# Attention and two dense layers on one core: two shared buffers for the raw rows of q, k and v, and phi written in place

## The chip, the core and the metric

The kernel runs on one core of a Trainium2 chip. The core has TensorE (PE in the profile; PEld are its weight loads), VectorE (DVE), ScalarE (ACT), GpSimd (POOL) and SyncE (SP), which here issues nearly all transfers, one after the other in a fixed order. Each engine works through its own list of instructions in order; an instruction that waits holds up all that stand behind it on that engine. The metric is the device time of one execution in microseconds (us).

## The reference

```python
B, H, S, D = 4, 8, 576, 64            # q, k, v: float32
scores = softmax(causal(q @ k.T / sqrt(D)))          # per batch and head
local  = scores @ v
q_p    = phi(q)                        # phi(x) = x + 1 for x > 0, exp(x) otherwise
mem    = (q_p @ M_prev) / (q_p . z_prev + 1e-6)
x      = g * mem + (1 - g) * local     # g = sigmoid(beta), per head
x      = x.transpose(0, 2, 1, 3).reshape(2304, 512)
h      = softplus(x @ w_in)  @ w_out   # 512 -> 2048 -> 512, weights float64
out    = relu(h @ w2_in) ** 2 @ w2_out # 512 -> 2048 -> 512, weights float64
```

All inputs but the float64 weights are float32. The kernel keeps every operand of a product as two 16-bit halves, a high one and a low one (the rest), and makes each product of three partial ones.

## The kernel before

The 2304 tokens are cut into 18 chunks of 128 (`NC`, `CH`): two batches run in turn, 4 chunks of each, and the two last half chunks of the pair form one mixed chunk; so chunks 0 to 8 are the first pair, 9 to 17 the second. Within a chunk the heads are taken in groups (`steps`), fewer groups where the row of scores is short.

For each chunk raw rows of k, q and v are loaded from HBM by SyncE (`load`, 256 KB each) and prepared. `prep_k`: ScalarE copies to 16 bits (L226), VectorE makes the low half (L227), a transposing transfer issued by SyncE writes `KT` (L193). `prep_q` does the same for `qT` (L217, L218), `prep_v` makes `V` without a transpose (L234, L235), and `prep_phi` makes `phi(q)` (L251, L252, L254) and its halves (L256, L257) and has them transposed into `phiT`. There are nine buffers each for `KT` and `V` (`KVB`), two each for `qT` and `phiT`. Raw rows of q, of k and of v have one buffer each; a second one, in another pool, holds the raw k of chunk 1. A raw row can be loaded once the row before it in its buffer has been used.

The attention of a group: scores on TensorE (L309), a VectorE reduction with the mask (L314), Exp on ScalarE (L318), the probabilities split into halves (L330 on ScalarE, L331 on VectorE) in one of two tiles `p16`, and transposed by a transfer into `PT` (L193; in chunks 0 and 1 TensorE transposes). Then TensorE multiplies with `M` (L346) and `V` (L354) into the one tile `pvt`, which VectorE scales (`xt`, L374; the tile has the tag `prod`, one buffer, which the first half of `prep_phi` uses too, as `phie`), adds (L381) and splits (L386, `xn`) into x, again transposed.

The first dense layer needs x of two chunks (a block of 256 tokens). Its weights come in 32 pieces of 512 KB (`wst`, three buffers), which VectorE turns from float64 to float32 and splits with four instructions each (L417, L418, L419, L422) and ScalarE with one (L421). `unit_h` makes 24 products (L434 to L436) and softplus (ScalarE L438 to L440, L444; VectorE L441, L445); `unit_xq` and `unit_x` the second product (L451 to L453, L496 to L498). These units are interleaved with the attention steps, by the costs in `unit_time` and `step_cost`. The second layer follows when attention is done; its weights are loaded and split in the same way from then on (`w34_to`).

The order of the instructions on every engine is fixed when the kernel is built: a scheduler takes ready work by priority (`tc.high_priority` raises attention and weights; the preparation of chunks has none) along a modelled timeline, in which a tile's buffers and their users count. So a change of buffers moves instructions on all engines.

Of the kernel before, what the change touches and what calls it, by code (L numbers as in the profile page):

```python
# [8 lines left out]
F32 = mybir.dt.float32  # L9
# [8 lines left out]
P = 128  # L18
# [20 lines left out]
NST = 3  # L39
PTB = 4  # L40
PB = 2
P16 = 2
ST2 = 4

# [2 lines left out]
def kernel(  # L47
# [16 lines left out]
    B, H, S, D = q.shape  # L64
# [46 lines left out]
    att = att_cm.__enter__()  # L111
# [4 lines left out]
    stage = stage_cm.__enter__()  # L116
# [18 lines left out]

    p16 = [att.tile([P, 2 * EMAX], F16, name=f"p16_{i}") for i in range(P16)]
    zero = stage.tile([P, P], F16, name="zero", bufs=1)
# [22 lines left out]
    raw, qT, phiT, KT, V, Mt, Pt, PT, pvt, cs_t = ({} for _ in range(10))  # L160

    def segs(g):
        x = CH[g]
        if len(x) == 2:
            return [(x[0], P * x[1], 0, P)]
        return [(2 * x[0] + i, 4 * P, i * R, R) for i in range(2)]

    def lo_eng(g):
        return dve if g < LOE else pool

    def load(nm, g, pool_=None):
        if g >= NC or (nm, g) in raw:
            return
        src = {"q": q, "k": k, "v": v}[nm]
        t = (pool_ or att).tile([P, H, D], F32, name="raw" + nm, bufs=1)
        for b, s0, r0, n in segs(g):
            sp.dma_start(out=t[r0:r0 + n], in_=src[b, :, s0:s0 + n, :].rearrange("h p d -> p h d"))
        raw[nm, g] = t
    def load_m(g):
        for b, s0, r0, n in (segs(g) if g < NC else []):  # L180
            if s0 == 0:
                t = att.tile([P, EMAX], F32, tag="Pt", name="mraw", bufs=PB)[:, :HD].rearrange("p (h d) -> p h d", h=H)
                for i in range(2):
# [3 lines left out]
    def transp(g, out, in_, lim):  # L187
        nblk = in_.shape[1] // P
        if g >= lim:
            step = nblk if nblk <= 12 else nblk // 2  # L190
            for a in range(0, nblk, step):
                e = a + step
                sp.dma_start_transpose(out=out[:, a:e], in_=in_[:, a * P:e * P])  # L193
            return
        for a in range(0, nblk, 8):
            e = min(nblk, a + 8)
            ps = mm.tile([P, 8, P], F16, tag="mm", name="tps")
            for i in range(a, e):
                pe.transpose(ps[:, i - a], in_[:, i * P:(i + 1) * P], ident)
            act.activation(out[:, a:e], ps[:, :e - a], AF.Copy)  # L200
# [47 lines left out]
    def prep_phi(g):  # L248
        r = raw.pop(("q", g))
        e = att.tile([P, H, D], F32, tag="prod", name="phie")  # L250
        act.activation(e, r, AF.Relu, scale=-1.0)  # L251
        act.activation(e, e, AF.Exp, scale=-1.0)  # L252
        f = att.tile([P, H, D], F32, name="phi")
        dve.scalar_tensor_tensor(f, r, 0.0, e, ALU.max, ALU.add)  # L254
        fn = att.tile([P, H, 2, D], F16, name="phin")
        act.activation(fn[:, :, 0, :], f, AF.Copy)  # L256
        lo_eng(g).tensor_tensor(fn[:, :, 1, :], f, fn[:, :, 0, :], ALU.subtract)  # L257
        phiT[g] = att.tile([P, H, P], F16, name="phiT", bufs=2)
        transp(g, phiT[g], fn.rearrange("p h t d -> p (h t d)"), TP)
# [24 lines left out]
    def emit_s(g, h0):  # L284
        G, ext = GRP[g], EXT[g]
        p = att.tile([P, EMAX], F32, name="Pt", bufs=PB)
        if h0 == 0:
# [219 lines left out]


    load("k", 0)
    load("q", 0)  # L510
    load("k", 1, stage)
    load("v", 0)
    gates()
    z_setup()
# [5 lines left out]
    def prep_part(g, part):  # L520
        if g >= NC:
            return
        if part == 0:
            prep_k(g)
            load("k", g + 1)
        elif part == 1:
            prep_q(g)
        elif part == 2:
            prep_phi(g)
            load("q", g + 1)  # L530
        elif part == 3:
            prep_v(g)
            load("v", g + 1)
            prep_m(g)
            load_m(g + 1)

    prep_k(0)
    prep_q(0)
    prep_phi(0)
    load("q", 1)  # L540
    prep_v(0)
# [344 lines left out]
```

## Time and profile before

| | us |
|---|---|
| median of 3 runs (976.44 to 980.92) | 976.58 |
| profiled execution, whole | 977.68 |
| its span, first to last instruction | 975.9 |
| PE busy | 884.2 (91%) |
| DVE busy | 668.0 (68%) |
| ACT busy | 587.2 (60%) |

The span is what the trace covers; the rest of the profiled execution, 1.8 us, lies around it. Busy shares are averages over stages: in the first tenth of the span PE is less than half busy, after it over nine tenths. A wait is idle time of an engine in front of an instruction, put down to what ended last of all that this instruction waited for; with engines that work in order, the work named can itself have been late for another reason, which its own wait shows. A DMA share of 1 means that on average all 16 DMA engines had packets under way; as packets overlap, it can pass 1.

### The profile page before, as it was taken

The page shows a single profiled execution, that of the slowest core. Times are in us where ns is not written, and L with a number is a line of the kernel's source. Part 1 is how long each engine was busy: PE and PEld are TensorE (multiplying, and loading weights), DVE is VectorE, ACT ScalarE, POOL GpSimd, SP SyncE. Part 2 cuts the span into 40 slices and gives each one's busy share as a digit, 9 for nine tenths or more (in the row PEclk, how much of TensorE's full clock was granted, in tenths as well). Part 3 has the DMA queues.
Part 4 walks back from the last instruction along what each step waited for, and adds up shares of the span by engine and source line. Part 5 has one row for each costly group of instructions (what it writes and reads, how often), then busy time and mean ns, then how long its engine had stood idle before and what let it go on. Part 6 is the DMA issues. An engine that isn't in the chain of part 4 may idle for free.

```text
span 975.9 us, 21791 instructions
## 1 busy us (share of the span) xinstructions
PE 884.2 (91%) x8994; PEld 680.1 (70%) x9012; DVE 668.0 (68%) x1437; ACT 587.2 (60%) x1094; POOL 2.2 (0%) x10
## 2 busy tenths in 40 slices
PE   4345898889998899999999999999999999999998
PEld 3234787778877788888888888544684585486483
DVE  7998998877748677675846499998894075066050
ACT  7765878768649687775937556562274065056051
POOL 0000000000000000000000000000000000000000
PEclk8555999999999999999999999999999999999999
DMA  9999989755699976646554375620000000000000
GB/s 232 224 241 215 214 162 195 118 95 112 99 159 176 160 125 104 104 83 108 94 88 80 64 234 172 211 65 22 22 2 11 33 1 4 30 12 1 33 12 22
DMA packets 283219, 101.05 MB, mean 104 GB/s; under 512 B 248048, under 2 KB 280816, under 8 KB 283120
## 3 DMA queue, kind: packets, MB, share of 16 engines
q1 hardware_dynamic: 282880, 99.65, 51.3%
q8 instruction: 70, 1.15, 0.5%
q14 instruction: 29, 0.24, 0.1%
q10 hardware_dynamic: 240, 0.02, 0.0%
HBM read 48.78 MB, written 4.72 MB: 55 GB/s over the span
## 4 chain that ended last, share of the span: by engine, by line
PE 60%; DMA 16%; DVE 13%; ACT 6%; issue 3%; SPq 1%; ACTq 0%; DVEq 0%
DMA PT<-p 8%; PE ops L829 7%; PE ops L827 6%; PE ops L828 6%; PE h2ps L801 4%; PE h2ps L799 4%; PE h2ps L800 4%; DMA rawq<-in_q_dram 3%; PE xps L452 3%; PE xps L451 3%; PE xps L453 3%; PE s_ps L309 3%; PE pvt L354 2%; PE hps L436 2%; PE hps L435 2%
## 5 line engine op out<-in xcount | busy, mean ns | idle before, releaser
L434 PE MATMUL hps<-x,W 128*128 128x256 f16 x576 | 157.8, 276 | 3.2 <-DVE cc L273 3.0
L435 PE MATMUL hps<-x,W 128*128 128x256 f16 x576 | 158.4, 276 | 1.7 <-ACT x L477 1.7
L436 PE MATMUL hps<-x,W 128*128 128x256 f16 x576 | 158.2, 275 | 0.0
L452 PE MATMUL xps<-g,W 128*128 128x256 f16 x512 | 138.5, 273 | 1.7 <-DVE g L445 1.7
L453 PE MATMUL xps<-g,W 128*128 128x256 f16 x512 | 138.7, 273 | 0.0
L451 PE MATMUL xps<-g,W 128*128 128x256 f16 x512 | 137.5, 273 | 1.1 <-DVE spa L441 0.7
L318 ACT ACTIVATE Pt<-Pt,cs 128x128 f32<-128x128 f32 (+4 forms) x144 | 84.2, 585 | 67.4 <-DVE cs L314 67.4
L309 PE MATMUL s_ps<-KT,qT 128*128 128x128 f16 (+2 forms) x992 | 83.9, 225 | 36.6 <-DVE cs L314 35.9
L829 PE MATMUL ops<-W,gg 128*128 128x512 f16 x288 | 108.5, 379 | 0.9
L827 PE MATMUL ops<-W,gg 128*128 128x512 f16 x288 | 109.2, 379 | 0.1
L828 PE MATMUL ops<-W,gg 128*128 128x512 bf16 x270 | 102.3, 379 | 0.0
L309 PEld LDWEIGHTS <-qT 128*128 128x128 f16 (+1 forms) x992 | 59.8, 105 | 48.5 <-issue 43.7
L331 DVE TENSOR_TENSOR p<-Pt,p 128x512 f16<-128x512 f32 (+2 forms) x104 | 69.3, 667 | 29.6 <-ACT p L330 28.8
L831 ACT ACTIVATE osb<-ops 128x512 f32<-128x512 f32 x18 | 10.8, 597 | 123.4 <-PE ops L829 123.4
L808 DVE TENSOR_TENSOR r<-h2ps,r 128x512 f32<-128x512 f32 (+1 forms) x16 | 10.0, 623 | 108.0 <-PE h2ps L801 107.2
L354 PE MATMUL pvt<-V,PT 128*128 128x64 f16 (+1 forms) x1392 | 60.7, 197 | 19.5 <-DMA PT<-p 18.3
L314 DVE CUSTOM_DVE_ANT_0 Pt<-s_ps,mask 128x128 f32<-128x128 f32 (+3 forms) x128 | 62.0, 485 | 18.6 <-PE s_ps L309 17.9
L354 PEld LDWEIGHTS <-PT 128*128 128x128 f16 (+1 forms) x1392 | 50.3, 104 | 28.7 <-DMA PT<-p 25.1
L330 ACT ACTIVATE p<-Pt 128x512 f16<-128x512 f32 (+2 forms) x104 | 63.1, 606 | 11.2 <-DMA PT<-p 10.2
L435 PEld LDWEIGHTS <-W 128*128 128x128 f16 x576 | 56.9, 99 | 10.2 <-issue 3.6
L799 PE MATMUL h2ps<-XT,WS 128*128 128x256 f16 (+1 forms) x256 | 63.7, 259 | 0.0
L800 PE MATMUL h2ps<-XT,WS 128*128 128x256 f16 (+1 forms) x256 | 63.7, 259 | 0.0
(160 smaller groups left out, 2076.5 us busy)
## 6 DMA issues: line engine op xcount, KB each, us to landing
wst<-in_moe_w_in_dram SPq DMA_DIRECT2D x32, 512.0 KB, 5.0
wst<-in_moe_w_out_dram SPq DMA_DIRECT2D x32, 512.0 KB, 4.7
rawk<-in_k_dram SPq DMA_DIRECT2D x16, 256.0 KB, 4.3
rawq<-in_q_dram SPq DMA_DIRECT2D x16, 256.0 KB, 3.9
rawv<-in_v_dram SPq DMA_DIRECT2D x16, 256.0 KB, 4.7
out_dram<-osb SPq DMA_DIRECT2D x16, 256.0 KB, 2.0
PT<-p SPq DMA_TRANSPOSE x100, 3.4
mraw<-in_M_prev_dram SPq DMA_DIRECT2D x8, 128.0 KB, 3.7
```

The source lines that it names most:

```text
L309: pe.matmul(o[x * n:(x + 1) * n], qT[g][:, t * H + h, x * n:(x + 1) * n], KT[kb][:, h, a - j * P:e - j * P], start=(t == 0), stop=(t == 1),)
L354: pe.matmul(o[r], t[:, o0 + i + y, r], V[kb][:, z, h, :], start=(i == 0 and y + z == 0), stop=(i == nb - 1 and y > 0),)
L434: pe.matmul(o, wh, x[:, c], start=(c == 0), stop=False)
L435: pe.matmul(o, wh, x[:, NCC + c], start=False, stop=False)
L436: pe.matmul(o, wl, x[:, c], start=False, stop=(c == NCC - 1))
L451: pe.matmul(ps, wh, gh, start=(f == f0), stop=False)
L452: pe.matmul(ps, wh, gl, start=False, stop=False)
L453: pe.matmul(ps, wl, gh, start=False, stop=(f == f1 - 1))
L799: pe.matmul(o, wh, xh, start=(k == 0), stop=False)
L827: pe.matmul(ps, gh, W4[0][:, f, :], start=(a == 0), stop=False)
L828: pe.matmul(ps, gh, W4[1][:, f, :], start=False, stop=False)
L829: pe.matmul(ps, gl, W4[0][:, f, :], start=False, stop=(a == NFC - 1))
```

## The change

Raw rows of q, k and v are allocated from one tag with two buffers (`RAWB`), in the order in which the program asks for them: k0, q0, k1, v0, q1, v1, and then k, q, v of each chunk. Each load takes the buffer of the raw row two places earlier and waits until that one has been used. The extra buffer for the raw k of chunk 1 is gone. `phi` is written over its input `phie`, so the buffer of the tag `prod` stays taken until both halves of phi are made, and not only until phi is. All else is as it was.

```diff
--- before.py
+++ after.py
@@ -39,6 +39,7 @@
 NST = 3
 PTB = 4
 PB = 2
+RAWB = 2
 P16 = 2
 ST2 = 4
 
@@ -168,11 +169,11 @@
     def lo_eng(g):
         return dve if g < LOE else pool
 
-    def load(nm, g, pool_=None):
+    def load(nm, g):
         if g >= NC or (nm, g) in raw:
             return
         src = {"q": q, "k": k, "v": v}[nm]
-        t = (pool_ or att).tile([P, H, D], F32, name="raw" + nm, bufs=1)
+        t = att.tile([P, H, D], F32, tag="raw", name="raw" + nm, bufs=RAWB)
         for b, s0, r0, n in segs(g):
             sp.dma_start(out=t[r0:r0 + n], in_=src[b, :, s0:s0 + n, :].rearrange("h p d -> p h d"))
         raw[nm, g] = t
@@ -250,7 +251,7 @@
         e = att.tile([P, H, D], F32, tag="prod", name="phie")
         act.activation(e, r, AF.Relu, scale=-1.0)
         act.activation(e, e, AF.Exp, scale=-1.0)
-        f = att.tile([P, H, D], F32, name="phi")
+        f = e
         dve.scalar_tensor_tensor(f, r, 0.0, e, ALU.max, ALU.add)
         fn = att.tile([P, H, 2, D], F16, name="phin")
         act.activation(fn[:, :, 0, :], f, AF.Copy)
@@ -508,7 +509,7 @@
 
     load("k", 0)
     load("q", 0)
-    load("k", 1, stage)
+    load("k", 1)
     load("v", 0)
     gates()
     z_setup()
```

What the change does to the lists of instructions (line numbers of the changed kernel are one higher from `RAWB` on).

SyncE, around the transposes of the first probabilities (`PT`) of chunk 2; `wst` are weight pieces. Before:

```order
36 L193 DMA_TRANSPOSE KT<-kn 128x8x128
37 L193 DMA_TRANSPOSE PT<-p_1_102 128x8x128
38 L177 DMA rawv<-in_v_dram 128x8x64
39 L177 DMA rawk<-in_k_dram 128x8x64
40 L401 DMA wst<-in_moe_w_out_dram 128x4x128
41 L193 DMA_TRANSPOSE PT<-p_0_101 128x8x128
42 L401 DMA wst<-in_moe_w_out_dram 128x4x128
43 L177 DMA rawq<-in_q_dram 128x8x64
44 L177 DMA rawv<-in_v_dram 128x8x64
45 L193 DMA_TRANSPOSE KT<-kn 128x8x128
46 L177 DMA rawk<-in_k_dram 64x8x64 x2
47 L398 DMA wst<-in_moe_w_in_dram 128x4x128
```

Now:

```order
36 L194 DMA_TRANSPOSE KT<-kn 128x8x128
37 L194 DMA_TRANSPOSE PT<-p_1_102 128x8x128
38 L402 DMA wst<-in_moe_w_out_dram 128x4x128
39 L194 DMA_TRANSPOSE qT<-qn 128x8x128 x2
40 L194 DMA_TRANSPOSE PT<-p_0_101 128x8x128
41 L178 DMA rawv<-in_v_dram 128x8x64
42 L399 DMA wst<-in_moe_w_in_dram 128x4x128 x2
43 L194 DMA_TRANSPOSE phiT<-phin 128x8x128
44 L194 DMA_TRANSPOSE PT<-p_1_102 128x8x128
45 L178 DMA rawk<-in_k_dram 128x8x64
46 L399 DMA wst<-in_moe_w_in_dram 128x4x128
47 L194 DMA_TRANSPOSE PT<-p_0_101 128x8x128
```

Before, raw v of chunks 6 and 7 and raw k of chunks 7 and 8 (two halves) stood here among the transposes; now it is raw v of chunk 4 and raw k of chunk 5, and one weight piece more. Over the whole list up to the transposed x of chunk 2, SyncE issues raw k for 11 chunks before and 7 now, raw v for 10 and 6, raw q for 6 and 6, `KT` transposes 7 and 4, weight pieces 22 and 25.

VectorE, at the first evaluation of softplus (`spa`, L441 before, L442 now) and behind it; `xt` is scaled attention output, `phin` the low half of phi. Before:

```order
236 L418 SCALAR_TENSOR_TENSOR wcv<-wst,wcv 128x512
237 L254 SCALAR_TENSOR_TENSOR phi<-rawq,phie 128x512
238 L372 TENSOR_TENSOR cc<-cc,gP 128x4
239 L418 SCALAR_TENSOR_TENSOR wcv<-wst,wcv 128x512
240 L273 TENSOR_SCALAR cc<-nps 128x2x4
241 L419 SCALAR_TENSOR_TENSOR wcv<-wst,wcv 128x512
242 L441 SCALAR_TENSOR_TENSOR spa<-hps,spa 128x512
243 L314 ISA Pt,cs<-s_ps,mask 128x384
244 L314 ISA cs 128x1
245 L374 TENSOR_TENSOR xt<-pvt,cc 128x512
246 L419 SCALAR_TENSOR_TENSOR wcv<-wst,wcv 128x512
247 L257 TENSOR_TENSOR phin<-phi,phin 128x8x64
```

Now (the row of phi itself, L255, stands four rows ahead of the first one shown):

```order
245 L423 TENSOR_TENSOR W_69<-wcv,W_68 128x4x128
246 L371 TENSOR_SCALAR cc<-cs 128x4
247 L276 TENSOR_TENSOR cc<-cc,gM 128x2x4
248 L332 TENSOR_TENSOR p_1_102<-Pt,p_1_102 128x2x256
249 L258 TENSOR_TENSOR phin<-phie,phin 128x8x64
250 L420 SCALAR_TENSOR_TENSOR wcv<-wst,wcv 128x512
251 L418 TENSOR_SCALAR wcv<-wst 128x512
252 L315 ISA Pt,cs<-s_ps,mask 128x384
253 L315 ISA cs 128x1
254 L372 RECIPROCAL cc<-cc 128x4
255 L446 TENSOR_TENSOR g_0_888<-spa,g_0_887 128x512
256 L375 TENSOR_TENSOR xt<-pvt,cc 128x512
```

Before, `xt` stood between phi and `phin`; now it follows `phin`. The first L441 has 243 instructions ahead of it in both lists; among them are 8 fewer of L227 and L235 now (halves of k and v), 7 more on weights, 1 fewer of L331, 3 more for q (L218 to L220), and small ones. The low half of x of chunk 1 (L386), on which the first dense unit waits, is instruction 209 before and 211 now: 6 fewer halves of k and v and 7 more on weights stand ahead of it, and one small one of 4 columns.

SyncE once more, where the second pair of batches begins, at the transposed x of chunk 10. Before:

```order
166 L193 DMA_TRANSPOSE x_2699<-xn 128x8x128
167 L193 DMA_TRANSPOSE KT<-kn 128x8x128
168 L177 DMA rawq<-in_q_dram 128x8x64
169 L177 DMA rawv<-in_v_dram 128x8x64
170 L177 DMA rawk<-in_k_dram 128x8x64
171 L193 DMA_TRANSPOSE qT<-qn 128x8x128 x2
172 L177 DMA rawv<-in_v_dram 128x8x64
173 L193 DMA_TRANSPOSE PT<-p_1_102 128x8x128
174 L193 DMA_TRANSPOSE KT<-kn 128x8x128
175 L177 DMA rawk<-in_k_dram 64x8x64 x2
176 L177 DMA rawv<-in_v_dram 64x8x64 x2
177 L193 DMA_TRANSPOSE phiT<-phin 128x8x128
```

Now:

```order
168 L194 DMA_TRANSPOSE x_2692<-xn 128x8x128
169 L178 DMA rawv<-in_v_dram 128x8x64
170 L194 DMA_TRANSPOSE qT<-qn 128x8x128 x2
171 L178 DMA rawk<-in_k_dram 128x8x64
172 L194 DMA_TRANSPOSE PT<-p_1_102 128x8x128
173 L178 DMA rawq<-in_q_dram 128x8x64
174 L194 DMA_TRANSPOSE KT<-kn 128x8x128
175 L194 DMA_TRANSPOSE phiT<-phin 128x8x128
176 L194 DMA_TRANSPOSE PT<-p_0_101 128x8x128
177 L194 DMA_TRANSPOSE x_2692<-xn 128x8x128
178 L194 DMA_TRANSPOSE PT<-p_1_102 128x8x128
179 L194 DMA_TRANSPOSE PT<-p_0_101 128x8x128
```

Before, the last raw k and v of all were loaded here (chunk 17, in halves); now it is raw v of chunk 14 and raw k and q of chunk 15. Between the transposed x of chunk 7 and that of chunk 10 SyncE issues raw k, v and q for 18 chunks in all before and for 13 now, and `KT` transposes 9 and 6.

## Rows read from the trace of the kernel before

**Rows 1.** By stretch: PE, PEld, DVE, ACT, POOL busy us; clock; DMA share; GB/s.
```profile
0.00:12.00 12.00, 3.06 (x34) 2.77 (x34) 5.92 (x15) 7.12 (x12) 2.24 (x10) 1.00 0.90 194
12.00:88.00 76.00, 33.22 (x350) 24.92 (x347) 72.36 (x200) 55.29 (x128) 0.00 (x0) 0.54 1.15 234
88.00:112.00 24.00, 19.06 (x205) 15.53 (x204) 19.78 (x54) 17.17 (x36) 0.00 (x0) 0.82 1.09 223
112.00:275.00 163.00, 150.23 (x2032) 131.77 (x2030) 133.75 (x308) 121.73 (x244) 0.00 (x0) 0.99 0.74 133
275.00:350.00 75.00, 67.30 (x823) 59.18 (x821) 51.80 (x144) 52.59 (x121) 0.00 (x0) 1.00 1.05 172
350.00:600.00 250.00, 242.26 (x3067) 213.96 (x3065) 171.48 (x390) 175.79 (x353) 0.00 (x0) 1.00 0.56 110
600.00:976.00 376.00, 369.03 (x2500) 231.95 (x2516) 212.90 (x331) 157.54 (x204) 0.00 (x0) 1.00 0.11 36
```

**Rows 2.** The tile of x (xn): first and last start of TensorE's transposes.
```profile
L199 PE MATMUL tps<-ident,xn x16: 267/314/314, 65.1 to 87.8; 128*128 128x128 f16 x16
```

**Rows 3.** Waits of VectorE, 12 to 88 us: us in total, times, longest.
```profile
DVE qn L218 <- ACT qn L217: 1.8, 2, 1.2
DVE kn L227 <- ACT kn L226: 1.8, 4, 0.7
DVE V L235 <- ACT V L234: 0.4, 1, 0.4
```

**Rows 4.** Waits of VectorE, 88 to 112 us.
```profile
DVE p L331 <- ACT p L330: 3.3, 1, 3.3
DVE kn L227 <- ACT kn L226: 1.0, 1, 1.0
```

**Rows 5.** Waits of TensorE, 88 to 112 us.
```profile
PE hps L434 <- DVE cc L273: 3.0, 1, 3.0
```

**Rows 6.** Groups by line: count, busy us, mean ns, idle before.
```profile
L418 DVE SCALAR_TENSOR_TENSOR wcv<-wst,wcv 128x512 int32<-128x512 int32 x64 | 43.9, 686 | 0.2
...
L227 DVE TENSOR_TENSOR kn<-rawk,kn 128x512 f16<-128x512 f32 x18 | 12.4, 689 | 5.5 <-ACT kn L226 5.5
```

**Rows 7.** Waits of ScalarE, 12 to 112 us.
```profile
ACT kn L226 <- DMA rawk<-in_k_dram: 6.6, 6, 2.4
ACT qn L217 <- DMA rawq<-in_q_dram: 4.9, 4, 2.4
ACT p L330 <- DMA PT<-p: 4.4, 2, 3.4
ACT V L234 <- DMA rawv<-in_v_dram: 2.5, 2, 2.3
```

**Rows 8.** DMA issues, 0 to 112 us: count, KB each, median us to landing.
```profile
wst<-in_moe_w_out_dram SPq DMA_DIRECT2D x10, 512.0 KB, 6.0
...
rawk<-in_k_dram SPq DMA_DIRECT2D x10, 256.0 KB, 4.6
rawv<-in_v_dram SPq DMA_DIRECT2D x9, 256.0 KB, 5.0
...
PT<-p SPq DMA_TRANSPOSE x9, 4.9
```

**Rows 9.** Waits of TensorE, 275 to 350 us.
```profile
PE pvt L354 <- DMA PT<-p: 5.4, 4, 2.3
```

**Rows 10.** DMA issues, 275 to 350 us.
```profile
rawv<-in_v_dram SPq DMA_DIRECT2D x7, 256.0 KB, 4.1
rawk<-in_k_dram SPq DMA_DIRECT2D x6, 256.0 KB, 4.1
rawq<-in_q_dram SPq DMA_DIRECT2D x3, 256.0 KB, 4.0
...
PT<-p SPq DMA_TRANSPOSE x9, 4.3
```

**Rows 11.** Waits of TensorE, 350 to 600 us.
```profile
PE pvt L354 <- DMA PT<-p: 6.2, 9, 1.1
```

**Rows 12.** Waits of TensorE for the tile xt, whole span.
```profile
PE pvt L346 <- DVE xt L374: 2.4, 3, 1.2
```

## The prediction

> **What bounds the kernel now.** I read the busy times by stretch first. In each row I subtract a column from the length to get the idle time of that engine. From 112 us on, TensorE is busy 150.2 of 163, 67.3 of 75, 242.3 of 250 and 369.0 of 376 us: it idles 12.8, 7.7, 7.7 and 7.0 us, and it sets the end [rows 1]. Ahead of 112 us it is otherwise: TensorE idles 8.9, 42.8 and 4.9 us in the first three rows, while VectorE is busy 72.4 of 76 us between 12 and 88 and the DMA share stands at 1.15. The first dense unit needs x of chunks 0 and 1, and the last transpose for that starts at 87.8 us [rows 2]. So there are two regimes: VectorE, fed by a full set of DMA engines, decides when the dense work starts; afterwards TensorE decides, and only its gaps can be won or widened.
>
> Next the waits in each regime. VectorE's idle 3.6 us between 12 and 88 us has some 4.0 us of waits beside it, all for raw rows by way of ScalarE's copy: 1.8 for q, 1.8 for k, 0.4 for v [rows 3]. From 88 to 112 us it waits 1.0 us for a raw k and 3.3 us for a copy of probabilities [rows 4], which itself waits for a `PT` transfer: ScalarE's waits there are 6.6 + 4.9 + 2.5 = 14.0 us for raw rows and 4.4 us for `PT` [rows 7]. TensorE's largest wait just after the dense work has begun, 3.0 us [rows 5], is put down to a VectorE instruction, so a late VectorE reaches TensorE here. From 275 to 350 us, where raw k and v of the second pair are fetched at a stroke, the DMA share is 1.05 again [rows 1], and 5.4 of the 7.7 us that TensorE idles are waits for `PT` [rows 9]. After that, 6.2 of 7.7 us are [rows 11].
>
> **The change part by part.** *VectorE's work ahead of the dense start.* The low half of x of chunk 1 has 6 fewer halves of k and v ahead of it and 7 more weight instructions. At 0.689 and at most 0.686 us each [rows 6] that is -4.1 and +4.8 us: at most +0.7, and nearer zero, since two of the seven at most are the shorter L417. The first softplus instruction has equally many ahead of it; there 8 halves go (-5.5 us) and 7 weight and 3 q instructions come (at most +6.9), less one of L331. What preparing less far ahead frees is taken by weights at once. I count 0, with -1 to +1.5 as bounds. The weights so made earlier buy nothing by themselves, for no TensorE wait between 88 and 112 us names them [rows 5], and the sum over both kinds up to their last piece is the same.
>
> *Raw rows and VectorE's waits in the front.* Up to the x of chunk 2, 27 raw rows are loaded before and 19 now. If each costs what it does now, 5.0 us of VectorE waits over 27, the 8 that go take 1.5 us along. But all three kinds now stand in a ring of two buffers, and k has been a one-buffer chain before: its waits are 1.8 + 1.0 = 2.8 us for about 10 rows, 0.28 us each. If every row is fetched that way, 19 cost 5.3 us, +0.3. I take the middle, -0.6, with -5.0 (no wait is left) below and +9 (worked out under the second rival) above.
>
> *Transfers in the front.* The same list has 8 rows of 0.262 MB and 3 `KT` transposes of the same size fewer and 3 weight pieces of 0.524 MB more. At the 234 GB/s of the stretch a row takes 1.12 us and a piece 2.24: -12.3 + 6.7 = -5.6 us of transfer. The stretch with rows and transposes and no weights moves only 172 GB/s at a full share [rows 1], 1.52 us a row; at that rate it is -16.7 + 6.7 = -10. Of 112 us these are 5 and 9%. `PT` lands in 4.9 us here and in 4.3 us in the later crowd [rows 8, 10]; the wait of 3.3 us [rows 4] is what a shorter queue could shorten. I take -0.5, with 0 and -3.3 as ends. Front together: -1.1.
>
> *The middle, 275 to 350 us.* Between the x of chunk 7 and that of chunk 10, 13 raw rows and 6 `KT` now stand where 18 and 9 stood. Eight transfers of 1.52 us are 12 us of a stretch of 75 that is full. The wait for `PT` is 5.4 us; TensorE gets back between nothing (`PT` is late for other reasons) and all of it. I take -2, as the crowd shrinks by a sixth and waits in a full queue fall faster than its length.
>
> *Later.* The 5 rows and 3 transposes arrive between 350 and 600 us instead, at a share of 0.56 [rows 1]: 12 us in 250, 5% more traffic. TensorE's 6.2 us of waits for `PT` grow by 5 to 15%, 0.3 to 0.9; I take +0.8, with 0 and +3 as ends. `KT` and `V` themselves are not late there: chunk 15's raw k is asked for when chunk 10 is done.
>
> *phi in place.* No instruction goes or comes. `xt` now has to wait until `phin` has been made; in the order it is moved behind it, with some ten instructions between phi and `xt` of which most stand ahead of `xt` anyhow. Behind `xt` TensorE's next `pvt` is queued, and through that everything on TensorE. All waits of that kind are 2.4 us in three now [rows 12], in the busy front; if `xt` came one instruction of phi (0.69 us, about the mean of [rows 6]) later in each of these three and in the next three, it would cost 4. Where dense units stand ahead, nothing. I take +0.3, between 0 and +4.
>
> Sum: 0 - 1.1 - 2 + 0.8 + 0.3 = -2.0 us. Against the profiled execution of 977.7 us (span 975.9 and 1.8 around it) that is 975.7. The median of the runs is 1.1 us below that execution, so I forecast 974.6 us on its scale.
>
> **The rivals.** *Faster: the crowd was the bound.* If the raw rows five chunks ahead are what delays the transfers that count, the front loses most of its 8.3 us of VectorE waits [rows 3, 4], say 5, and the middle its whole 5.4: -10.4, with the later +0.8 -9.6, 967 us. For it speaks that `PT` lands later where shares are above 1 [rows 8]; against it, that weight pieces fill the room in the front and that a third of ScalarE's wait for raw rows is for q [rows 7], which the new order does not fetch less of. A rule of the Trainium skill bears on this, "DMA: Bandwidth & Descriptors", Specifications: transfers need about 512 bytes a piece for full rate. The rows' 172 against 234 GB/s agree in direction. By that rule the freed time is the -10 and not the -5.6 us above, which raises this rival a little and is already an end of the term.
>
> *Slower: the ring shows each load.* With two buffers a raw row is asked for only when the one two places earlier has been used; transfer (4.6 to 5.0 us, [rows 8]), copy and half then stand in a line, and in the front ScalarE and VectorE wait in order with attention behind them. If each of the 19 rows cost ScalarE 2.1 us (the longest waits it has now are 2.3 and 2.4, [rows 7]), that is 40 us; VectorE has felt 5.0 of ScalarE's 14.0, 36%, so 14 instead of 5: +9. The middle, with 13 rows the same way, could give back its -2. 976.6 + 9 = about 985 us. It decides once VectorE's waits for raw rows ahead of 112 us pass 10 us. For it: this chain is the shape that k has already, and ten or so of ScalarE's waits come of it. Against it: the 27 rows went through such chains before too, in one buffer each, and 19 rows on two buffers in 112 us leave about 11.8 us a turn, over twice a landing. The Trainium skill speaks for this rival: "Perfetto Trace Analysis", Optimization Strategy, says that a repeated gap on the engine that should be busy can mean too few buffers for the next tile. By that rule gaps ahead of L226, L217 and L234 would now grow; how much, it does not say.
>
> *Nothing happens.* The weights take every slot that k and v leave, `PT` stays as late, and the time is that of before, 976.6. As a result it is hard to tell from the forecast.
>
> **How the numbers follow.** Forecast 0.42, nothing 0.14, faster 0.25, slower 0.19. A measurement of this kernel can tell about 0.5%, 4.9 us, from no change: 971.7 and 981.5 us are the borders. Faster: all of that rival and a little of the forecast's low end, from the wide ends of its terms, 0.31. Slower: that rival and the upper ends of phi and the ring, 0.23. Within: 0.46. The forecast's own range, from terms that err by 1 to 3 us each, is 970 to 980. For eight in ten I reach to 965.5 on one side, where the faster rival lies inside, and to 985 on the other.
>
> **What would show it.** Right: x of chunk 1 is ready between 84 and 89 us; VectorE's waits for raw rows ahead of 112 us stay between 3 and 6 us; the DMA share between 275 and 350 us falls to about 0.9, with `PT` waits of 3 to 4 us there; dense work ends attention with the same gaps after 350 us, plus or minus 2. Wrong: first dense products more than 3 us from where they were, waits on L217, L226 or L234 that have doubled, TensorE waits for `xt` above 5 us, or gaps ahead of scores for a `KT` that is late.

## The result, and the profile after

The changed kernel takes **986.7 us** (median of 6 runs, 984.3 to 990.7) against 977.7 us (6 runs, 976.4 to 980.9) for the kernel before on the same chip: a ratio of 1.0091, 95% interval 1.0063 to 1.0120. It is slower by about 9 us where 2 us less were forecast. The profiled execution took 987.0 us, its span is 985.2 (before: 975.9). Line numbers are one higher than before from L42 on.

Busy times by stretch of the changed kernel answer to [rows 1]:

```profile
0.00:12.00 12.00, 3.52 (x38) 3.07 (x38) 7.11 (x18) 7.32 (x13) 2.24 (x10) 1.00 0.88 214
12.00:88.00 76.00, 33.93 (x352) 24.71 (x351) 73.22 (x209) 55.16 (x126) 0.00 (x0) 0.62 1.01 226
88.00:112.00 24.00, 21.84 (x261) 18.73 (x260) 22.14 (x54) 16.48 (x35) 0.00 (x0) 0.91 1.04 197
112.00:275.00 163.00, 147.58 (x1979) 128.84 (x1977) 128.98 (x293) 120.12 (x242) 0.00 (x0) 0.97 0.77 139
275.00:350.00 75.00, 68.70 (x833) 60.12 (x832) 49.71 (x145) 54.95 (x126) 0.00 (x0) 0.98 0.80 145
350.00:600.00 250.00, 241.06 (x2988) 210.42 (x2986) 166.72 (x381) 169.37 (x341) 0.00 (x0) 0.99 0.60 114
600.00:976.00 376.00, 372.25 (x2536) 236.48 (x2553) 220.39 (x344) 163.03 (x214) 0.00 (x0) 1.00 0.12 38
```

Between 275 and 350 us the DMA share has fallen from 1.05 to 0.80, and TensorE idles 6.3 us there in place of 7.7. The loss does not stand in TensorE's idle time as a whole: over the whole span it idles as long as before (91.5 us, before 91.7), but its busy time has grown. On the two pages the same line reads, of before and then of after:

```profile
PE 884.2 (91%) x8994; PEld 680.1 (70%) x9012; DVE 668.0 (68%) x1437; ACT 587.2 (60%) x1094; POOL 2.2 (0%) x10
```

```profile
PE 893.7 (91%) x8994; PEld 684.3 (69%) x9012; DVE 668.3 (68%) x1437; ACT 587.0 (60%) x1094; POOL 2.2 (0%) x10
```

The same 8994 recorded products are busy 9.5 us longer. Two things in the rows make a product longer. One is the granted clock. Windows laid on three of the stretches in which it falls after the dense work has begun (last column but two):

```profile
123.20:126.60 3.40, 3.40 (x21) 2.40 (x17) 3.22 (x9) 1.60 (x4) 0.00 (x0) 0.50 0.87 194
...
290.40:293.80 3.40, 3.40 (x19) 2.42 (x17) 1.75 (x6) 1.29 (x4) 0.00 (x0) 0.50 0.68 150
539.60:543.00 3.40, 3.40 (x18) 2.31 (x18) 1.77 (x4) 0.14 (x1) 0.00 (x0) 0.50 0.00 0
```

0.50 is the 1.2 GHz level. Between 95 and 960 us the changed kernel has six such stretches of 3.4 us, 20.4 us together; before has two, at 103.5 and 195.7 us, 6.9 us together. Most of them come behind an idle TensorE, after 2.1 us up to 122.8 and 2.9 us up to 289.1 for instance; the one at 539.6 comes behind products as in the next rows. At half the clock a stretch does half its work, so on TensorE alone it costs half its length: 10.2 against 3.4 us. Whether the kernel pays that is a question for the experiments.

The other is a change of width. Where a score product with 64-column weights (a mixed chunk) stands between two dense ones, the timeline of TensorE in the changed kernel reads (start, length):

```profile
518.28 0.27 PE L437 MATMUL hps<-x,W 128*128 128x256 f16 x1
518.39 0.27 PE L435 MATMUL hps<-x,W 128*128 128x256 f16 x1
518.50 0.27 PE L436 MATMUL hps<-x,W 128*128 128x256 f16 x1
518.71 0.24 PE L310 MATMUL s_ps<-KT,qT 128*64 128x128 f16 x1
518.88 0.28 PE L437 MATMUL hps<-x,W 128*128 128x256 f16 x1
519.09 0.24 PE L310 MATMUL s_ps<-KT,qT 128*64 128x128 f16 x1
519.27 0.28 PE L435 MATMUL hps<-x,W 128*128 128x256 f16 x1
```

Dense products among themselves start 0.11 us apart; a dense and a narrow product together take 0.39 us, where 0.11 and the 0.056 us of a score product would make 0.17. That is 0.10 us a switch: 14.3 us in the changed kernel and 11.2 before, by the starts of its products, since its list has more switches (148 for 122).

The last transpose for x of chunk 1 starts at 85.3 us, before 87.8 [rows 2]:

```profile
L200 PE MATMUL tps<-ident,xn x16: 267/314/314, 65.0 to 85.3; 128*128 128x128 f16 x16
```

So the 9.3 us between the two spans are, in the trace's account: first dense product at 87.0 in place of 89.7 us, -2.7; TensorE's gaps above 0.35 us behind it 41.2 in place of 39.3, +1.9; switches +3.1; half clock +6.8; rest +0.2. This compares one traced execution with one other; it says where the time stands, and not what caused it.

TensorE's waits for `PT` from 112 to 275 and from 350 to 600 us are, in the changed kernel, 9.9 and 8.9 us (first two lines). Before they were 6.7 us (third line) and 6.2 [rows 11]. The last line is the changed kernel's from 275 to 350 us, where 5.4 stood [rows 9]:

```profile
PE pvt L355 <- DMA PT<-p: 9.9, 11, 2.1
...
PE pvt L355 <- DMA PT<-p: 8.9, 10, 1.9
...
PE pvt L354 <- DMA PT<-p: 6.7, 10, 1.2
...
PE pvt L355 <- DMA PT<-p: 3.7, 2, 2.9
```

VectorE's waits that follow raw rows, from 12 to 112 us, answer to [rows 3, 4]; they are 4.4 us together (before 5.0):

```profile
DVE qn L219 <- ACT qn L218: 2.6, 3, 1.6
DVE V L236 <- ACT V L235: 1.3, 2, 0.8
DVE kn L228 <- ACT kn L227: 0.5, 1, 0.5
```

ScalarE's own waits for raw rows in the same stretch answer to [rows 7]; they have grown from 14.0 to 19.2 us, those for v from 2.5 to 6.3:

```profile
ACT qn L218 <- DMA rawq<-in_q_dram: 7.4, 4, 3.7
ACT V L235 <- DMA rawv<-in_v_dram: 6.3, 2, 3.4
ACT kn L227 <- DMA rawk<-in_k_dram: 5.5, 4, 2.1
```

Last, SyncE's own waits at the line that loads raw rows, first of after (the three longest rows), then of before:

```profile
SPq L178 <- DVE kn L228: 6.7, 5, 2.1
SPq L178 <- DVE phie L255: 5.5, 5, 2.8
SPq L178 <- DVE cs L315: 5.1, 6, 1.7
```

```profile
SPq L177 <- DVE cs L314: 1.9, 4, 0.8
SPq L177 <- DVE phi L254: 1.9, 3, 1.3
SPq L177 <- DVE V L235: 1.8, 2, 1.4
```

All rows of this line added, SyncE stands 42.3 us in 48 waits at raw loads, before 18.8 us in 25; `PT` transposes stand behind them in its list.

### The profile page after: what moved, and what is told of

The parts are those of the page before. It is cut to its first block, busy times and chain, and to the rows that moved or that the text cites. A ratio compares the mean times of both kernels' runs of the same rounds, so it can differ in the third digit from the quotient of the medians.

```text
span 985.2 us, 21786 instructions
## 1 busy us (share of the span) xinstructions
PE 893.7 (91%) x8994; PEld 684.3 (69%) x9012; DVE 668.3 (68%) x1437; ACT 587.0 (60%) x1094; POOL 2.2 (0%) x10
## 4 chain that ended last, share of the span: by engine, by line
PE 58%; DMA 16%; DVE 13%; ACT 8%; issue 4%; SPq 1%; ACTq 0%; DVEq 0%
DMA PT<-p 8%; PE ops L830 7%; PE ops L828 6%; PE ops L829 6%; PE h2ps L802 4%; PE h2ps L800 4%; PE h2ps L801 4%; PE xps L453 3%; PE xps L452 3%; PE xps L454 3%; PE s_ps L310 3%; PE hps L436 3%; PE hps L437 2%; PE hps L435 2%; PE pvt L355 2%
## 5 line engine op out<-in xcount | busy, mean ns | idle before, releaser
L435 PE MATMUL hps<-x,W 128*128 128x256 f16 x576 | 159.3, 279 | 1.4 <-DMA x<-xn 1.4
L436 PE MATMUL hps<-x,W 128*128 128x256 f16 x576 | 160.0, 278 | 0.0
L437 PE MATMUL hps<-x,W 128*128 128x256 f16 x576 | 159.9, 278 | 0.0
L310 PE MATMUL s_ps<-KT,qT 128*128 128x128 f16 (+2 forms) x992 | 87.6, 226 | 30.7 <-DVE cs L315 30.3
L355 PE MATMUL pvt<-V,PT 128*128 128x64 f16 (+1 forms) x1392 | 59.0, 197 | 22.5 <-DMA PT<-p 22.5
L355 PEld LDWEIGHTS <-PT 128*128 128x128 f16 (+1 forms) x1392 | 49.5, 103 | 30.5 <-DMA PT<-p 27.7
L331 ACT ACTIVATE p<-Pt 128x512 f16<-128x512 f32 (+2 forms) x104 | 63.1, 607 | 8.9 <-DMA PT<-p 7.4
```

What stands on the lines that cost most here:

```text
L310: pe.matmul(o[x * n:(x + 1) * n], qT[g][:, t * H + h, x * n:(x + 1) * n], KT[kb][:, h, a - j * P:e - j * P], start=(t == 0), stop=(t == 1),)
L355: pe.matmul(o[r], t[:, o0 + i + y, r], V[kb][:, z, h, :], start=(i == 0 and y + z == 0), stop=(i == nb - 1 and y > 0),)
L435: pe.matmul(o, wh, x[:, c], start=(c == 0), stop=False)
L436: pe.matmul(o, wh, x[:, NCC + c], start=False, stop=False)
L437: pe.matmul(o, wl, x[:, c], start=False, stop=(c == NCC - 1))
```

## The experiments

Times are medians; the ratio is to the kernel before as timed beside it, with its 95% interval. Half-clock time is that of the trace's clock record between 95 and 960 us. A trace shows one execution. Code is shortened: `...` marks what is left out, and a statement of several lines stands on one. In the expectations ORDER, RING, PHI and so on name rival explanations, and a width switch is a change between 64- and 128-column weights in TensorE's list.

**The parts alone, and one buffer more.** phi_only is the kernel before with the one line of phi; ring_only the changed kernel without it; ring3 the changed kernel with three buffers.

```diff
-        f = att.tile([P, H, D], F32, name="phi")
+        f = e
...
-RAWB = 2
+RAWB = 3
```

> phi in place alone, raw rows as before. Three theories. ORDER (the theory): the change costs nothing by its buffers, but by the TensorE list that it moves: each change between 64-wide and 128-wide weights costs 0.10 us (57 cost 5.7 us between 485 and 620 us before, 95 cost 10.1 us after), and each fall of the granted clock 1.7 us (six falls after, two before). This list has 138 such changes against 122 before and 148 after: +1.6 us, and 0 to 4 falls more or fewer: 976 to 986 us. RING (rival): the loads wait for two shared buffers; without the ring as before, 977.7 us, within 2. PHI (rival): xt kept behind phin is the cost; 984 us or more, with waits for xt above 5 us.

> Two shared buffers for the raw rows, phi in a tile of its own as before. ORDER: 116 changes of weight width in the TensorE list, 6 fewer than before: -0.6 us, and the front 2 us earlier as after; falls of the clock two to six: 974 to 982 us. RING: as after, 985 to 989 us, with VectorE's waits for raw rows as there. PHI: as before, within 2 of 977.7 us.

> Three shared buffers instead of two, phi in place. ORDER: 108 changes of width, 40 fewer than after: -4 us of them, and the clock falls about as often as chance has it, two to six times: 975 to 984 us. RING: a third buffer takes most of the exposure away: 979 us or less, and then the waits of ScalarE for raw rows ahead of 112 us (20 us after) are nearer to or below the 15 of before. PHI: as after, 985 to 989 us.

phi_only 985.2 us, 1.0071 (1.0048 to 1.0094); ring_only 984.3, 1.0047 (1.0023 to 1.0070); ring3 **967.9**, 0.9889 (0.9855 to 0.9923), which beats both kernels; its trace shows no half clock between 95 and 960 us, and ScalarE's waits for raw rows ahead of 112 us are 8.0 us there. Each part costs by itself, and together (9.1 us) they cost less than their sum (6.8 and 5.9). In its trace phi_only starts its dense work at 95.6 us in place of 89.7: TensorE waits between 88 and 112 us for the x of chunk 1.

```profile
PE hps L434 <- ACT x L200: 5.4, 1, 5.4
```

Its waits for `xt` are 4.0 us, before 2.4 [rows 12], and not the 5 that PHI named. The traced execution took 978.5 us, the shortest of 12: with the late start it is only 0.8 us longer than the traced one of before. So the late start is not shown to be what the other 6 us come from.

**Scores of a mixed chunk kept together** (after_grp): order-only ties between a chunk's score products and the dense units, 94 switches in the list.

```diff
+    tc.add_manual_dep(m.ins, prev[-1].ins.name, DependencyInfo(NoSync, DATA), reason="scores together")
```

> The changed kernel, both parts, with an order on TensorE alone (no wait) that keeps the scores of a mixed chunk together: the first product of such a head group stands behind the last dense unit asked for, and the next unit's first product behind the scores. Buffers, loads and phi as after. ORDER: 94 changes of width against 148 of after: -5 us, and the fall of the clock at 540 us, in the stretch of single alternations, goes: -1.7. 979 to 981 us, with falls elsewhere 977 to 984. RING and PHI: as after within 2, 985 to 989 us.

985.6 us, 1.0074 (1.0049 to 1.0099), 1 us less than the changed kernel and within its interval. The switches did shrink from 14.3 to 7.6 us, but gaps grew by 6.0: what TensorE saves there, it waits.

**Held lists.** The scheduler makes new lists for each set of buffers. In the next kernels every engine's instructions are tied in the order of the changed kernel, so that one thing alone differs.

```diff
+    for x, y in zip(line, line[1:]):
+        tc.add_manual_dep(y, x.name, DependencyInfo(NoSync, DATA), reason="list")
```

ring3_list_after has three buffers, ring_only_list_after two and a phi tile of its own.

> Three shared buffers with phi in place, as in the 967.9 us kernel, but every engine's instructions held in the order in which they stand in the changed kernel (986.7 us). Only the room for raw rows differs from the changed kernel, only the order from the 967.9 us one. ORDER (the order of the lists makes the time, by clock falls and weight-width switches): 982 to 989 us, VectorE's and ScalarE's waits for raw rows shorter without gain. RING (the loss is loads waiting for one of two buffers): 966 to 979 us.

> Two shared buffers and all lists held as in the changed kernel, but phi has a tile of its own. Only the wait of xt for phin is gone. PHI (phi in place costs time at a held order): 980 to 984 us. ORDER and QUEUE: 986.7 us, plus or minus 2, as neither the lists nor the room for raw rows differ.

ring3_list_after takes 980.3 us, 1.0016 (0.9996 to 1.0036); this interval does not touch the changed kernel's. So at one and the same order the third buffer is worth 6.4 us by the medians and 7.3 by the ratios, between both expectations. Its half-clock time is that of the changed kernel or more (23.9 us, for 20.4). TensorE's gaps, counted as above, are 35.6 us in place of 41.2, which is nearly all of the 5.8 us between the two traced spans. Its `PT` waits between 112 and 600 us are 17.1 us, for 22.5; those between 112 and 350 us are 9.0, for 13.6:

```profile
PE pvt L436 <- DMA PT<-p: 9.0, 11, 2.6
```

```profile
PE pvt L355 <- DMA PT<-p: 13.6, 13, 2.9
```

SyncE's list shows one way in which this comes about. The changed kernel, and below it the one with three buffers (lines 81 higher):

```profile
428.59 1.25 SPq L194 DMA_TRANSPOSE PT<-p  x1
431.13 1.28 SPq L178 DMA_DIRECT2D rawq<-in_q_dram  x2
432.46 1.35 SPq L194 DMA_TRANSPOSE KT<-kn  x1
433.92 2.09 SPq L194 DMA_TRANSPOSE PT<-p  x1
```

```profile
423.14 1.25 SPq L275 DMA_TRANSPOSE PT<-p  x1
424.49 1.28 SPq L259 DMA_DIRECT2D rawq<-in_q_dram  x2
425.87 1.30 SPq L275 DMA_TRANSPOSE KT<-kn  x1
427.37 1.21 SPq L275 DMA_TRANSPOSE PT<-p  x1
```

The same four entries: the first `PT` leaves 5.45 us later with two buffers, the raw q 6.64, the `KT` and `PT` behind it 6.59 and 6.55. SyncE stood still ahead of the raw q (from 429.84 to 431.13 us) and not with three buffers, and TensorE then waits for the last of these `PT`, first line, where with three it comes without a wait:

```profile
437.66 0.43 PE L355 MATMUL pvt<-V,PT 128*128 128x64 f16 x9 [0.59 <-DMA PT<-p]
...
431.58 0.43 PE L436 MATMUL pvt<-V,PT 128*128 128x64 f16 x9
```

The same happens near 282 us. It is not the whole: the longer wait at 263 us (1.9 us, for 0.6) is for a `PT` that has no such delay ahead of it and takes 5.4 us to land, for 4.1. And how long SyncE stands at raw loads is no price in itself: it is 7.0 us here in place of 42.3, but 45.2 us in ring3, the fastest kernel of all. ScalarE's waits for raw rows between 112 and 470 us are nearly equal, 10.5 us with three buffers and 11.6 with two. ring_only_list_after: 986.5 us, 1.0082 (1.0053 to 1.0111): at this order phi in place costs nothing that can be told.

**Idle time filled** (after_fill, lists held).

```diff
+FILL = {(4, 2): 60, (6, 1): 65, (6, 3): 40, (8, 2): 55, (8, 7): 85, (14, 1): 55}
...
+            pe.matmul(o, phiT[g][:, h], Mt[b][:, 0, h, :], start=True, stop=True).ins
+            for _ in range(FILL.get((g, h), 0))
```

> The changed kernel with all lists held as they stand there, and 24 to 85 more products of 64 columns (0.029 us each, written where a later product overwrites them) put into TensorE's list at six places where it stands idle for 1.6 to 3.1 us, near 120, 188, 198, 261, 286 and 423 us; they are meant to end before the wait does. CLOCK (the half-clock stretches at 123, 191, 201 and 290 us come from these idle times and cost half their length): those four stretches go, 6.8 us less, minus up to 1.5 us where the products last longer than the wait: 979 to 982.5 us. If the half-clock stretches cost nothing or come of something else: 986.7 us to 992 (the products together last 10.4 us, and what does not fit in a wait is added).

987.2 us, 1.0085 (1.0060 to 1.0110): a miss. Three of the four stretches are gone, half clock 10.2 in place of 20.4 us, and at 126 us TensorE is 3.6 us ahead. At 337 us it is 1.0 us behind, and from 343 on 2 to 6: it has the products added, and other waits for `PT` have come, 2.2 us up to 345.8 and 2.1 up to 423.6 among them. (The traced execution, 991.2 us, is the longest of six.) The half-clock account above is where the time stands, not what its removal gives back. Nor does half-clock time rank the kernels: the traced executions of before_hs and ring3_hs, below, have 13.7 us of it each, with spans of 972.7 and 968.8 us, beside 6.8 and 0 us in before (975.9) and ring3 (967.8).

**A gap made on purpose** (ring3_gap: ring3 with held lists, six stops of TensorE ahead of row tiles of the last layer).

```diff
+            more.append(pe.matmul(ps[:, :64], Z[:, :P], Z[:, :64], start=True, stop=True).ins)
+            for _ in range(4):
+                pool.memset(Z, 0.0)
+            more.append(pe.matmul(ps[:, :64], Z[:, :P], Z[:, :64], start=True, stop=True).ins)
```

> The 967.9 us kernel (three shared buffers), its lists held, with TensorE stopped six times ahead of a row tile of the last layer, where nothing else makes it wait: each time one small product, four GpSimd memsets of 128x512 (about 2 us), one small product. That work is added and changes no output. Without an effect on the clock: six gaps of 2.2 to 2.8 us, 967.9 + 13 to 17 = 981 to 985 us, and no half-clock stretch after 91 us. CLOCK: a stretch of about 3.4 us at 1.2 GHz behind most of the gaps, 1.7 us each: 8 to 10 us more, 990 to 995 us.

990.2 us, span 989.4: 21.6 more than ring3. Each stop takes 2.64 us. The first two rows stand around one; the product behind it is followed by products 0.43 us apart, and from 654.4 us by such 0.22 us apart:

```profile
648.43 0.19 PE L909 MATMUL ops<-Z 128*128 128x64 f16 x1
651.02 0.23 PE L912 MATMUL ops<-Z 128*128 128x64 f16 x1 [2.39 <-POOL Z L911]
651.07 0.61 PE L917 MATMUL ops<-W,gg 128*128 128x512 f16 x1
651.47 0.63 PE L920 MATMUL ops<-W,gg 128*128 128x512 bf16 x1
651.90 0.63 PE L921 MATMUL ops<-W,gg 128*128 128x512 f16 x1
...
654.40 0.38 PE L921 MATMUL ops<-W,gg 128*128 128x512 f16 x1
654.62 0.38 PE L917 MATMUL ops<-W,gg 128*128 128x512 f16 x1
```

Three of the six equal gaps were followed by 3.4 us at half clock (at 650.9, 743.1 and 855.7 us), three by none. The last layer begins 0.5 us later than in ring3 and ends 21.6 us later; of the 21.1 us between, 6 x 2.64 = 15.8 are the stops, and the other 5.2 are 1.7 for each fall, its half length. Here, where nothing else makes TensorE wait, a fall costs its price in full. Ahead of the last layer it did not: this trace has 10.2 us of half clock there (at 152.6 and 521.2 us) and ring3's has none, and yet the layer begins only those 0.5 us later.

**Other lists for the same buffers.** The scheduler's preference for score steps at 110 or 120.

```diff
-HS = 100
+HS = 110
```

> The changed kernel with the same buffers; only the scheduler's preference for score steps is 110 in place of 100, which puts 4405 of the 9012 products at another place of TensorE's list (104 width switches in place of 148). RING: 986.7 us, plus or minus 2, as no buffer differs. ORDER: another time by at least 3 us in either direction, 974 to 984 us by the switches alone (44 x 0.10 us = 4.4 less, and up to 6 by falls); and the span less half of its half-clock time after the first dense product comes out at 971 us, plus or minus 3, as in the six kernels so far (967.8 to 972.3).

> The kernel before, buffers unchanged, with the scheduler's preference for score steps at 110 in place of 100. RING, QUEUE, PHI: the time of before, plus or minus 2, since nothing about rows or phi differs. ORDER (a moved list alone changes the time by several us): off by 3 us or more, likelier above (142 width switches in place of 122: +2; falls of the clock unknown, 0 to 6 of 1.7 us): 976 to 988 us.

> The kernel before with only phi made in place (985.2 us), with the preference for score steps at 110 in place of 100 (110 width switches in place of its 130). If those 985.2 us are the luck of one list: 976 to 981 us, as before with either preference (978.2, 979.3). If phi in place costs time by way of every list that the scheduler then makes: 983 to 988 us.

> The changed kernel with the preference at 120, a third list for two shared buffers (130 width switches). RING (room is what sets the level, the list moves it by 2 or 3 us): 982 to 989 us, beside 986.7 and 983.8. ORDER (a list can be lucky with two buffers too): 975 to 981 us.

> Two shared buffers, phi in a tile of its own, preference at 110 (112 width switches): the fourth corner of before, phi only, ring only and both under a second list. If two shared buffers cost by themselves, whatever the list: 982 to 987 us, as with the first list (984.3). If those 984.3 were one unlucky list: 976 to 981 us.

> Three shared buffers with phi in place and the preference at 110. If the gain of three buffers is their room: 966 to 971 us. ORDER: the 967.9 us of the first order were a list without a fall of the clock and with 1.7 us fewer switches; another list has 2 to 6 falls of 1.7 us: 971 to 979 us, still below the changed kernel's under either preference by the 6.4 us that the room was worth at a held order.

| buffers for raw rows, phi | preference 100 | 110 | 120 |
|---|---|---|---|
| one a kind, phi apart (before) | 1 | 1.0004 (0.9981 to 1.0028) | |
| one a kind, in place | 1.0071 | 1.0075 (1.0050 to 1.0099) | |
| two shared, apart | 1.0047 | 1.0101 (1.0062 to 1.0141) | |
| two shared, in place (after) | 1.0091 | 1.0054 (1.0034 to 1.0074) | 1.0128 (1.0096 to 1.0160) |
| three shared, in place | 0.9889 | 0.9906 (0.9873 to 0.9940) | |

A list moves a kernel by up to 0.7%, and the half clock with it; but no list of the five with two buffers, and none of the two with phi in place alone, reaches the kernel before. The slowdown is not one unlucky list. before_hs and ring3_hs came out as the rivals of ORDER had it (1.1 us from before, and within 966 to 971 us); after_hs stands at the edge of ORDER's range, and after_hs2 and ring_only_hs above every range. The rule named for after_hs, that the span less half of its half-clock time comes to 971 us, plus or minus 3, does not hold: counted in the same way it is 974.2 there, 964.1 in before_hs, 961.9 in ring3_hs and 987.2 in ring4. phi_only_hs starts its dense work at 95.5 us, as phi_only did. TensorE's `PT` waits between 112 and 600 us are 18.3 and 16.8 us in the lists of before, and 22.5 to 27.7 in those five with two buffers; but they are 21.0 us in ring3, so they do not rank the kernels across lists. (The traced execution of before_hs is the shortest of its 12, that of after_hs the longest of its 10.)

**By which path?** after_pool takes the raw loads out of SyncE's list and gives them to GpSimd's queue, in halves; after_late puts each two entries later in SyncE's list (lists held in both).

```diff
-            sp.dma_start(out=t[r0:r0 + n], in_=src[b, :, s0:s0 + n, :]...)
+                m = pool.dma_start(out=t[r0 + a:r0 + a + P // 2], in_=src[b, :, s0 + a:s0 + a + P // 2, :]...)
...
+            keys = [(i + 2 + 0.5 if x.name in names and i > 20 else i, i) for i, x in enumerate(line)]
+            line = [line[i] for _, i in sorted(keys)]
```

> The changed kernel with all lists held, but the loads of raw q, k and v rows leave by GpSimd's queue (two transfers of 64 rows each) and no longer stand in SyncE's, where they stood still for 42 us in 48 waits with PT transposes behind them (before: 19 us in 25). Buffers and the order on the other engines are those of the changed kernel. QUEUE (at one and the same order two buffers cost time because a load that waits for its buffer holds up the PT transposes behind it): 978 to 983 us, as with three buffers and the same lists (980.3), PT waits of TensorE between 112 and 350 us about 9 us in place of 13.6. RAW (the rows themselves come late): 985 to 989 us. A slower start by GpSimd's queue could add 1 to 2 us to either.

> The changed kernel with all lists held, except that in SyncE's list each load of a raw row stands two entries later, so behind one or two PT transposes or weight pieces that it stood ahead of; buffers unchanged. QUEUE (a load that waits for its buffer holds up the transposes behind it): SyncE's waits at raw loads fall from 42 us to 10 to 25, TensorE's PT waits between 112 and 350 us from 13.6 to 9 to 11, time 980 to 984 us. RAW (two buffers cost because rows come late): they come later still, ScalarE's and VectorE's waits for raw rows grow, 987 to 995 us.

1138.8 and 1092.6 us: both fail to tell the two apart. In after_late SyncE stands only 7.0 us at raw loads, yet rows come so late that ScalarE waits 60.6 us for v and 59.7 for k up to 600 us:

```profile
ACT V L316 <- DMA rawv<-in_v_dram: 60.6, 15, 7.3
ACT kn L308 <- DMA rawk<-in_k_dram: 59.7, 14, 7.0
```

Lateness of rows is thus dear here; but two and three buffers at held lists differ in `PT` and hardly in these waits. That the 6.4 us come by way of later `PT` is what the two traces say; that SyncE's list is what makes them late is seen in places, and no run shows it alone.

**More room still.** ring4 is RAWB = 4; ring3_phi has three buffers and a phi tile of its own.

> Four shared buffers, phi in place, preference at 100. RING: one more buffer takes waits away again: 963 to 968 us, at most as long as with three (967.9). ORDER: its list has 148 width switches as the changed kernel's, 4.9 us more than with three, and falls of its own: 970 to 976 us.

> Three shared buffers and phi in a tile of its own, preference at 100, a list of its own. If phi in place costs time by way of the lists wherever it is made (6.8 us with the buffers of before, 2.4 with two shared ones): 961 to 966 us. ORDER (the list decides, 150 width switches in place of 108 or so with three buffers and phi in place, 4 us more, falls unknown): 970 to 980 us. PHI at nothing and the room at its level: 966 to 971 us.

994.7 us, 1.0168 (1.0139 to 1.0197), and 991.1, 1.0120 (1.0101 to 1.0140): misses. Room alone does not set the level: with more room these two are about as slow as the slowest list with two buffers, or slower, so the table above cannot by itself put the slowdown on the room. What does is the pair at held lists. The list of the kernel before, held with two buffers, was not run. ring4 has 6.8 us of half clock only; it begins its dense work at 92.2 us, and its `PT` waits are 24.6 us. With ring3_list_after this says that of ring3's 18.8 us below the changed kernel 6.4 are the buffer at a held list and 12.4 the list that the scheduler then made (half clock 23.9 to 0 us, switches 14.2 to 9.8). Why the scheduler makes a good list for three buffers with phi in place, twice, and poor ones for its two neighbours stays open.

## Why the prediction was wrong, point by point

*VectorE's work and transfers in the front: right.* x of chunk 1 is transposed up to 85.3 us [rows 2], within 84 to 89; the first dense product comes 2.7 us earlier, where the sum had 1.1.

*Raw rows on VectorE: right in size.* 4.4 us, within 3 to 6. One sign of being wrong did come: ScalarE's waits for v have more than doubled. The slower rival named 10 us on VectorE as the point from which it decides. It was not reached, so that its time, 985 us, is nearly what came is luck: not by its path. The step that failed is in that rival and in the term beside it: **the ring's price was taken from ScalarE's and VectorE's waits alone, with "attention behind them"**, at -0.6 us in the sum. At held lists the room for a third row is worth 6.4 us, with nearly equal waits for raw rows on ScalarE behind 112 us, and with `PT` waits of TensorE 5.4 us apart between 112 and 600 us. The load itself waits too, and it does so in SyncE's list with `PT`, `KT` and x behind it; that is how some of those `PT` come late. How the others do stays open.

*The middle, 275 to 350 us: right.* Share 0.80 (about 0.9 was named), `PT` waits 3.7 us in place of 5.4, -1.7 where -2 was forecast.

*Between 112 and 275 us the sum has no term.* The raw k and v and the `KT` that the sum takes out of the front have to come there: before, none was issued in this stretch, now there are raw k and v of 4 chunks each and 3 `KT`. `PT` waits grew from 6.7 to 9.9 us, more than the middle gave back.

*Later: too small.* +0.8, with +3 as an end; 6.2 to 8.9 us is +2.7.

*TensorE's list and clock: left out.* Every term was counted in us of waiting, at full clock, by the premise that of TensorE's time "only its gaps can be won or widened", and its list behind 112 us was taken as if it stayed. In the profiled execution the half clock is +6.8 and the width switches +3.1 of the 9.3 us. The made gaps show that a fall is paid in the last layer; after_fill and after_grp show that either sum need not come back when its cause is taken away. That these two sums made the kernel slower is therefore not shown.

*phi in place: right here, wrong by itself.* +0.3 was forecast, 0 measured at a held order. Made alone it costs 6.8 and 8.0 us under two lists, beyond the end of 4. Both traces have a dense start 6 us later, where in the changed kernel it is earlier than before; by which path the cost comes stays open.

*Nothing happens, and the faster rival:* refuted. `PT` came later, not earlier, between 112 and 275 us.

## What to carry to other kernels

When buffers become fewer, ask in whose list the load waits for its buffer, and what stands behind it there: here VectorE, on which the prediction had put the price, hardly noticed, and TensorE waited longer for the transposes of another stage. The time that the queue stands at such loads is no price, for the fastest kernel has most of it. In a stretch where nothing else makes the engine that sets the end wait, a wait costs more than its length if the clock falls behind it; elsewhere taking away one cause showed the next wait. Where a scheduler makes the lists, hold them for one experiment, and make a second list for the same buffers, before a difference of 1% is put down to the buffers.

## What the hardware showed beside this

- Equal gaps of 2.6 us on a busy TensorE were followed by 3.4 us at 1.2 GHz three times in six; with that a stop of 2.64 us cost 4.4 us.
- Alternating 64- and 128-column weights costs 0.10 us a switch, while products with 128-column weights and 256 columns of data follow each other every 0.109 us.
- The same raw rows by GpSimd's queue, 36 transfers of 128 KB a kind at held lists, cost 152 us: 1138.8 against 986.7, with ScalarE waiting 74.9 us for v.
